# Attention's first three halves: plain fp32 products of unsplit q, k, probabilities and v, with both heads' products with v in column tiles of the array

## The chip, the cores and the metric

The kernel runs on one core of one Trainium2 chip. The metric is the device time of one execution in microseconds; runs are given as a median. PE is TensorE (PEld its weight loads), DVE VectorE, ACT ScalarE, POOL GpSimd, SP the engine that issues most DMAs.

## What is computed

Three stages follow each other on 4 x 768 = 3072 tokens: attention with sinks and a window, a feed-forward layer with a cosine, and a top-1 mixture of eight experts. All inputs are fp32.

```python
# attention: q, k, v are (4, 8, 768, 64); n_sink = 4, window = 128
scores = scale * np.matmul(q, k.transpose(0, 1, 3, 2))
keep = is_sink | in_window
a = softmax(np.where(keep, scores, -1e9))
x = np.matmul(a, v)                      # to (3072, 512)
# feed-forward, d_ff = 2048
h = x @ w_in
x = (h * np.cos(h)) @ w_out
# experts, 8 of width 1024
e = argmax(x @ w_gate + modality_bias[modality_id])
out = gate_w * (np.maximum(x @ w1[e], 0) @ w2[e])
```

## The kernel before, in words

**Halves and pairs.** Attention is worked in eight halves `hb` of 384 queries each (batch `hb // 2`, first or second part of its sequence `hb % 2`), and each half in four pairs of heads (`pr`), two heads of 64 side by side on the 128 partitions. A half has three query tiles `t` of 128. A tile sees its own block of 128 keys, the block before it, and 16 sink columns: 272 columns, and 128 for the very first tile of a sequence. A second half loads four key blocks, a first half three.

**Split products.** Matmuls work on the type fp32r, which rounds its operands. To keep fp32 precision each operand is written as a high part (ACT copies it into an fp32r tile) and a low part (DVE or POOL subtracts the high part from the value), and three products are summed in PSUM: high x high, high x low, low x high. This is done for the weights and activations of all three stages, and in attention for q, k, the probabilities and v. The transposes through PE (against `ident`) are of plain fp32, and so is the small product `pf` that spreads reciprocal sums (`mm(pf, rb[t], ident)`), which has no low parts.

**The steps of a pair** (`attn_front`, from L404):
- front: loads of q and k (L428, L429); `pq`: three transposes of q, `qT_h` by ACT and `qT_l` by DVE (L464); `pk`: transposes of k, `kT_h` by ACT (L486) and `kT_l` by DVE, then the sink keys copied behind each block (L489, L490).
- `load_v` (L431): v of the pair and its 16 sink rows `vs_n` (L436, L438). `split_v` (L494): high parts of v and of the sink rows by ACT (L497, L499), low parts by POOL, into `vp` and `vs`.
- `mid` (L515): the scores. For each tile three products per head (L136 is the helper `mm`, all products of attention and of `hp` have that line), the two heads on rows 0 to 63 and 64 to 127 of the array; DVE masks, scales and finds the row's extreme (L548), ACT takes the exponential with the row sum (L564).
- `rest` (L567): transposes of the probabilities `pt` (L588, L589), `pT_h` by ACT (L592), `pT_l` by DVE; the sink columns likewise through `pz` (L613) into `sp`; then the products with v into one PSUM bank `po`: two for the sinks and three for each block and head, with weights 128 columns wide in which the other head's 64 columns are zero. At the end the result is normalised and split into `xT_h` and `xT_l`, the input of the feed-forward stage.

From half 3 on (`STACK = 3`, L37) attention uses another, "stacked" form of these products; halves 0 to 2 use the form just described. In halves 0 and 1 the odd pairs (`extra`) hold q, k, v and the probabilities in tiles that later serve as weights of the feed-forward layer.

**Order of the work.** The feed-forward layer (`ffn_tile_gen`) runs in tiles of 384 tokens, 16 blocks `f` per tile, each of 12 products `hp` of 384 columns and 12 products `y` of 512 columns (L688); tile 0 does six blocks at first. `attn_half` (L365) yields steps with planned costs (`STEPS_0`, `STEPS_1`), and the loop at the end of attention calls `run_ffn` (L1035) after each step, so that tile `hb - 1` is spread over half `hb`. Halves 0 and 1 are piped (`PIPX`): `merge` (L342) mixes the rest of a pair with the scores of the next. Into the same order `conv_gen` (L281) weaves the conversion of the feed-forward weights, which come as 64-bit numbers: 32 blocks, each with one load by SP, work of ACT (L268, L306) and four DVE instructions (L140, L145, L148), the last of them as late as half 2. Each engine works its own queue in order, and SP issues its loads and stores in order too.

Of the kernel before, what the change touches and what calls it, by code (L numbers as in the profile page):

```python
# [11 lines left out]
F32 = DT.float32  # L12
# [8 lines left out]
P = 128  # L21
# [40 lines left out]
def kernel(  # L62
# [84 lines left out]
    def tt(e, o, a, b, op):  # L147
        e.tensor_tensor(out=o, in0=a, in1=b, op=op)  # L148
# [96 lines left out]
    kl = [kT2[:, 1]]  # L245
    ks = apool.tile([P, NPAIR, 2, NS], F32, name="ks")
    v_form = [False]
    DVE.memset(vs_n, 0.0)
    DVE.memset(vs.bitcast(F32), 0.0)
    DVE.memset(vp[:, :, D:5 * D].rearrange("p t (x d) -> p t x d", d=D)[:, :, 0:4:3].bitcast(F32), 0.0)  # L250
    POOL.memset(sp[4 * NS:].bitcast(F32), 0.0)

# [151 lines left out]
    def attn_front(hb, pr):  # L404
# [5 lines left out]

        whole = hb > EX
        n_ps = [0]

# [28 lines left out]
        qT_h = apool.tile([P, HALF], F32R, name="qT_h")  # L442
        qT_l = apool.tile([P, HALF], F32R, name="qT_l")
# [4 lines left out]
        stack = hb >= STACK  # L448
        hr = [slice(0, D), slice(D, 2 * D)]
        kT_h, kT_l = kT2[:, 0], kT2[:, 1]  # L450
        if stack:

            qT = [qT_h, qT_l]
            kx = late_pool().tile([P, 4, SEG], F32R, name="kx")
            kT = [kT_h, kx]
            if len(kl) == 1:
                kl.append(late_pool().tile([P, 4, SEG], F32R, name="kT_l1"))
                for j in range(2):
                    POOL.memset(kl[j][hr[1 - j]].bitcast(F32), 0.0)
# [10 lines left out]
        pk3 = pk.rearrange("p (t s) -> p t s", s=P)  # L470
        bs = [P, 2, nblk - 1, NS]
# [22 lines left out]
        def split_v():  # L494
            vp4 = vp.rearrange("p t (x d) -> p t x d", d=D)
            if not stack:
# [4 lines left out]
                return  # L501
            if not v_form[0]:
                v_form[0] = True
                POOL.memset(vp4[:, :, 2].bitcast(F32), 0.0)
                POOL.memset(vs[0:4 * NS].bitcast(F32), 0.0)
            ACT.activation(out=vp4[:, 0:nblk, 1:4:2, :], in_=vn[:, 0:nblk], func=AF.Copy)
# [8 lines left out]
        def mid():  # L515
            nonlocal mx, sm, Pb, Pt, cols
            kTh = kT_h.rearrange("p t s -> p (t s)")
            kTl = kT_l.rearrange("p t s -> p (t s)")
            if extra:
# [12 lines left out]
            def scores(t, js):  # L532
# [34 lines left out]
        def rest():  # L567
# [11 lines left out]
            yield steps(hb)[3]  # L579
            pT_h = apool.tile([P, 2, NQ * 256], F32R, name="pT_h")  # L580
            pT_l = apool.tile([P, 2, NQ * 256], F32R, name="pT_l")
            for t in range(NQ):
# [7 lines left out]
                oh = pT_h[:, :, t * 256 + s0:(t + 1) * 256]  # L590
                ol = pT_l[:, :, t * 256 + s0:(t + 1) * 256]
# [20 lines left out]
            for t in range(t0, NQ):  # L612
                PE.transpose(pz[0:2 * NS, t * P:(t + 1) * P], pc[:, t].rearrange("p j s -> p (j s)"), ident)  # L613
            sh, sl = sp[0:2 * NS], sp[2 * NS:4 * NS]
            if half == 0 and pr == 0:

                POOL.memset(sp[0:4 * NS, 0:t0 * P].bitcast(F32), 0.0)
            ACT.activation(out=sh[:, t0 * P:], in_=pz[0:2 * NS, t0 * P:HALF], func=AF.Copy)
            tt(DVE, sl[:, t0 * P:], pz[0:2 * NS, t0 * P:HALF], sh[:, t0 * P:].bitcast(F32), ALU.subtract)
            yield steps(hb)[5]  # L620
# [9 lines left out]
            if not stack:  # L630

                po = psb("po")
                mm(po[:, 0:HALF], vs[:, 0:2 * D], sp, True, False)
                mm(po[:, 0:HALF], vs[:, 2 * D:4 * D], sp, False, False)
                for j in range(2):
                    for blk in range(nblk):
                        c0, c1, m0, m1 = band(blk)
                        vh, vl = [vp[:, blk, (o + j) * D:(o + j + 2) * D] for o in (0, 3)]
                        mm(po[:, c0:c1], vh, pT_h[:, j, m0:m1], False, False)
                        mm(po[:, c0:c1], vh, pT_l[:, j, m0:m1], False, False)  # L640
                        mm(po[:, c0:c1], vl, pT_h[:, j, m0:m1], False, j == 1 and blk == nblk - 1)
                        yield steps(hb)[6]
                if whole:
                    ACT.activation(out=xh[:, pr, :], in_=po[:, 0:HALF], func=AF.Copy)
                    tt(DVE, xl[:, pr, :], po[:, 0:HALF], xh[:, pr, :].bitcast(F32), ALU.subtract)
                else:
# [7 lines left out]
                    tt(POOL, xl[:, pr, :], xs, xh[:, pr, :].bitcast(F32), ALU.subtract)  # L654
            if stack:
                xs = apool.tile([P, HALF], F32, name="xs")
            for j in range(2 if stack else 0):
# [241 lines left out]
    def late_pool():  # L899
        ypool_of()  # L900
        return ypl["late"]
# [546 lines left out]
```

## Time and profile before

| | us |
|---|---|
| median of 3 runs | 1201.5 (1201.12 to 1206.84) |
| the profiled execution | 1205.88 |
| its span, first to last instruction | 1204.0 |
| mean granted TensorE clock | 0.981 of 2.4 GHz |

Over the span PE is busy 1133.3 us (94%), PEld 1001.3, DVE 788.4 (65%), ACT 702.2 (58%), POOL 299.5 (25%). Matmuls are pipelined: a matmul's duration is longer than the distance to the next one's start, so busy time of PE says little about how much it could still take, and distances between starts say more. A row of a group gives the line, engine, operation, out<-in with shapes, the count, then busy time and mean ns of one, then the engine's idle time just before such instructions and who ended it. In the timeline the first two columns are the start and the time that the merged instructions cover, in us.

### The profile page before, as it was taken

The numbers are of one execution on the slowest core, as the hardware profiler recorded it, in microseconds if no ns is written. First come the engines' busy times: TensorE is split into PE (matmuls) and PEld (weight loads), VectorE is DVE, ScalarE is ACT, GpSimd is POOL, SyncE is SP. The second block draws the span as 40 slices with busy tenths as digits, with TensorE's granted clock in tenths as the row PEclk, the third lists the DMA queues.
The fourth block names the chain that finished last, engine by engine and source line by source line (L and its number), as shares of the span: only waits on it lengthen the run. The fifth ranks groups of instructions, "written<-read, shape, count | busy, mean of one in ns | idle before, by whom it ended". The sixth has DMA issues, their size and how long they took to land. (4 is left out here: it accounts for less than half of the span.)

```text
span 1204.0 us, 21827 instructions
## 1 busy us (share of the span) xinstructions
PE 1133.3 (94%) x6688; PEld 1001.3 (83%) x6688; DVE 788.4 (65%) x2293; ACT 702.2 (58%) x1453; POOL 299.5 (25%) x364
## 2 busy tenths in 40 slices
PE   5889889999999999999999999999999999999995
PEld 4777677798888898987889898989889988889984
DVE  7887879977788788788788777565762215622220
ACT  4678678777777788876788775334422225522221
POOL 1333333422322232222322222232221122122110
PEclk9889889999999999999999999999999999999998
DMA  5653456533333343333334324261333114211110
GB/s 138 159 166 117 126 167 190 149 84 79 83 93 85 78 115 79 96 95 75 75 94 114 85 54 132 78 220 54 97 130 126 38 54 137 77 53 57 37 39 24
DMA packets 141338, 118.87 MB, mean 99 GB/s; under 512 B 98415, under 2 KB 107631, under 8 KB 141168
## 3 DMA queue, kind: packets, MB, share of 16 engines
q1 hardware_dynamic: 136848, 103.29, 30.7%
q0 software_dynamic: 4320, 13.65, 3.5%
q8 instruction: 66, 1.08, 0.4%
q14 instruction: 104, 0.85, 0.3%
HBM read 151.32 MB, written 19.67 MB: 142 GB/s over the span
## 5 line engine op out<-in xcount | busy, mean ns | idle before, releaser
L148 POOL TENSOR_TENSOR g_l<-ch,g_h 128x384 fp32r<-128x384 f32 x128 | 132.0, 1032 | 424.4 <-ACT g_h L760 394.4
L136 PE MATMUL hp<-xT_h,wi_h 128*128 128x384 f32 x512 | 182.1, 356 | 0.0
L136 PE MATMUL hp<-xT_h,wi_l 128*128 128x384 f32 x512 | 174.6, 341 | 0.0
L136 PE MATMUL hp<-xT_l,wi_h 128*128 128x384 f32 x512 | 174.4, 341 | 0.0
L688 PE MATMUL y<-wo,g_h 128*128 128x512 f32 x384 | 161.0, 419 | 0.0
L688 PE MATMUL y<-wo_l,g_h 128*128 128x512 f32 x384 | 158.2, 412 | 0.0
L688 PE MATMUL y<-wo,g_l 128*128 128x512 f32 x384 | 155.9, 406 | 0.2 <-POOL g_l L148 0.2
L145 DVE SCALAR_TENSOR_TENSOR hT<-m_h,hT 128x256 fp32r<-128x256 f32 x88 | 37.3, 424 | 151.2 <-ACTq L1346 95.0
L136 PE MATMUL m_y<-wi_h,hT 128*128 128x512 f32 x416 | 132.4, 393 | 0.6 <-issue 0.4
L750 ACT ACTIVATE ch<-ch,cols 128x384 f32<-128x384 f32 x128 | 78.9, 616 | 85.2 <-DVE ch L145 84.0
L136 PEld LDWEIGHTS hp<-xT_h,wi_h 128*128 128x128 f32 x512 | 97.4, 190 | 4.9 <-issue 0.6
L142 DVE TENSOR_SCALAR ch<-hp 128x384 int32<-128x384 f32 x128 | 71.1, 555 | 45.1 <-PE hp L136 30.2
L136 PEld LDWEIGHTS hp<-xT_l,wi_h 128*128 128x128 f32 x512 | 97.5, 190 | 3.7 <-issue 0.4
L136 PEld LDWEIGHTS hp<-xT_h,wi_l 128*128 128x128 f32 x512 | 97.1, 190 | 0.6 <-issue 0.2
L136 PEld LDWEIGHTS m_y<-wi_h,hT 128*128 128x128 f32 x416 | 78.1, 188 | 16.9 <-issue 0.8
L564 ACT ACTIVATE Pb<-Pb,mx 128x272 f32<-128x272 f32 (+1 forms) x168 | 82.8, 494 | 12.7 <-DVE mx L548 12.0
L760 ACT ACTIVATE g_h<-ch 128x384 fp32r<-128x384 f32 x128 | 66.4, 519 | 40.5 <-DVE ch L148 32.0
L148 DVE TENSOR_TENSOR ch<-ch,hp 128x384 f32<-128x384 f32 x128 | 70.2, 550 | 28.4 <-ACT ch L750 26.8
L1163 ACT ACTIVATE hT<-m_h 128x256 fp32r<-128x256 f32 x88 | 33.8, 384 | 88.4 <-PE m_h L136 81.3
L688 PEld LDWEIGHTS y<-wo,g_l 128*128 128x128 f32 x384 | 73.3, 191 | 14.0 <-POOL g_l L148 0.6
L136 PE MATMUL m_y<-wi_l,hT 128*128 128x512 f32 x208 | 81.0, 390 | 0.0
L688 PEld LDWEIGHTS y<-wo,g_h 128*128 128x128 f32 x384 | 73.5, 192 | 8.7 <-issue 0.5
(306 smaller groups left out, 2821.8 us busy)
## 6 DMA issues: line engine op xcount, KB each, us to landing
rw<-in_moe_w_dram SPq DMA_DIRECT2D x112, 512.0 KB
wo_l<-wl_scr SPq DMA_DIRECT2D x122, 256.0 KB
cv_in<-in_moe_w_in_dram SPq DMA_DIRECT2D x16, 512.0 KB
cv_out<-in_moe_w_out_dram SPq DMA_DIRECT2D x16, 512.0 KB
y_scr<-yt SPq DMA_DIRECT2D x24, 256.5 KB
xT_h<-xg_h SPq DMA_DIRECT2D x32, 192.0 KB
xT_l<-xg_l SPq DMA_DIRECT2D x32, 192.0 KB
qn<-in_q_dram SPq DMA_DIRECT2D x56, 96.0 KB
```

Source lines behind the costliest of these rows:

```text
L136: PE.matmul(o, l, r, start=start, stop=stop)
L142: e.tensor_scalar(out=o, in0=i, scalar1=s1, scalar2=s2, op0=op0, op1=op1)
L145: e.scalar_tensor_tensor(out=o, in0=i0, scalar=s, in1=i1, op0=op0, op1=op1)
L148: e.tensor_tensor(out=o, in0=a, in1=b, op=op)
L564: ACT.activation(out=Pb[t][j][:, c0:c1], in_=Pb[t][j][:, c0:c1], func=AF.Exp, scale=-1.0, bias=mx[:, i:i + 1], accum_out=sm[:, i:i + 1])
L688: i = PE.matmul(o, l, r, start=start, stop=stop)
L750: ACT.activation(out=ch, in_=ch, func=AF.Sin, scale=TWO_PI, bias=half_pi)
L760: ACT.activation(out=gh, in_=ch, func=AF.Copy)
L1163: ACT.activation(out=hT_h[f], in_=hp, func=AF.Relu)
```

## The change

In halves 0, 1 and 2 (`stack` false) q, k, the probabilities, the sink columns and v stay whole, in fp32 tiles. Scores are one fp32 product per tile and head instead of three fp32r products. For the products with v the heads no longer share weights of 128 columns: head j has weights of 64 columns, `vn` as it was loaded, and writes partitions 64 j to 64 j + 63 of `po`. `split_v` does nothing in these halves. q, k, the probabilities and the sink rows have two buffers by turns (they use the places of the high and low tiles), v has three in the even pairs. The tiles of the stacked form are made when half 3 begins (`stacked`), in the same places. The yields keep their planned costs.

```diff
-    vp = apool.tile([P, 4, 6 * D], F32R, name="vp")
-    vs = apool.tile([P, 4 * D], F32R, name="vs")
-    vs_n = apool.tile([4 * NS, 2 * D], F32, name="vs_n")
-    sp = apool.tile([P, HALF], F32R, name="sp")
-    kT2 = apool.tile([P, 2, 4, SEG], F32R, name="kT_hl")
...
+    vs_n = apool.tile([P, 2 * D], F32, name="vs_n")
...
+    vn3 = apool.tile([P, 3, 4, 2, D], F32, name="vn3", tag="vp")
+    vs_n1 = apool.tile([P, 2 * D], F32, name="vs_n1", tag="vs")
+    spf = apool.tile([P, HALF], F32, name="spf", tag="sp")
+    kf2 = apool.tile([P, 2, 4, SEG], F32, name="kf", tag="kT_hl")
+    DVE.memset(vs_n1, 0.0)
+    POOL.memset(spf, 0.0)
+    st_ = {}
+
+    def stacked():
+        if not st_:
...
         def load_v():
           nonlocal vn
-          if not extra:
-              vn = apool.tile([P, 4, 2, D], F32, name="vn")
+          if vn is None:
+              vn = apool.tile([P, 4, 2, D], F32, name="vn") if stack else vn3[:, pr % 3]
           for j in range(2):
...
-            for g_ in range(2):
-                SP.dma_start(out=vs_n[(2 * g_ + j) * NS:(2 * g_ + j + 1) * NS, j * D:(j + 1) * D], in_=v[b, h0 + j, 0:NS, :])
+            for g_ in range(2 if stack else 1):
+                SP.dma_start(out=vn_s[(2 * g_ + j) * NS:(2 * g_ + j + 1) * NS, j * D:(j + 1) * D], in_=v[b, h0 + j, 0:NS, :])
...
+            qf = apool.tile([P, HALF], F32, name="qf", tag=("qT_h", "qT_l")[pr % 2])
+            kf_ = kf2[:, pr % 2]
...
-            ACT.activation(out=qT_h, in_=pq[:, 0:HALF], func=AF.Copy)
-            tt(DVE, qT_l, pq[:, 0:HALF], qT_h.bitcast(F32), ALU.subtract)
+            ACT.activation(out=qf, in_=pq[:, 0:HALF], func=AF.Copy)
...
-            ACT.activation(out=kT_h[:, 0:nblk, 0:P], in_=pk3[:, 0:nblk, :], func=AF.Copy)
-            tt(DVE, kT_l[:, 0:nblk, 0:P], pk3[:, 0:nblk, :], kT_h[:, 0:nblk, 0:P].bitcast(F32), ALU.subtract)
-            if half == 0:
-                DVE.tensor_copy(ks[:, pr], kT2[:, :, 0, 0:NS].bitcast(F32))
-            DVE.tensor_copy(kT2[:, :, 0:nblk - 1, P:SEG], ks[:, pr].unsqueeze(2).to_broadcast(bs))
+            ACT.activation(out=kf_[:, 0:nblk, 0:P], in_=pk3[:, 0:nblk, :], func=AF.Copy)
+            if half == 0 and hb + 1 < STACK:
+                DVE.tensor_copy(ks[:, pr, 0], pk3[:, 0, 0:NS])
+            if half == 0 and hb + 1 >= STACK:
+                DVE.tensor_copy(ks[:, pr, 0].bitcast(F32R), pk3[:, 0, 0:NS])
+                tt(DVE, ks[:, pr, 1], pk3[:, 0, 0:NS], ks[:, pr, 0], ALU.subtract)
+            src = pk3[:, 0:1, 0:NS] if half == 0 else ks[:, pr, 0:1, :]
+            DVE.tensor_copy(kf_[:, 0:nblk - 1, P:SEG], src.to_broadcast([P, nblk - 1, NS]))
...
         def split_v():
+            if not stack:
+                return
...
-                ACT.activation(out=vp4[:, 0:nblk, 0:3:2], in_=vn[:, 0:nblk], func=AF.Copy)
-                tt(POOL, vp4[:, 0:nblk, 3:6:2], vn[:, 0:nblk], vp4[:, 0:nblk, 0:3:2].bitcast(F32), ALU.subtract)
-                ACT.activation(out=vs[0:4 * NS, 0:2 * D], in_=vs_n, func=AF.Copy)
-                tt(POOL, vs[0:2 * NS, 2 * D:4 * D], vs_n[0:2 * NS], vs[0:2 * NS, 0:2 * D].bitcast(F32), ALU.subtract)
...
-                    for n_, (q_, k_) in enumerate(((qT_h, kTh), (qT_h, kTl), (qT_l, kTh))):
-                        for j in js:
-                            mm(ps[j][:, 0:w], q_[hr[j], qs], k_[hr[j], o:o + w], n_ == 0, n_ == 2)
+                    for j in js:
+                        mm(ps[j][:, 0:w], qf[hr[j], qs], kfr[hr[j], o:o + w], True, True)
...
-                ACT.activation(out=oh, in_=pt[:, :, s0:256], func=AF.Copy)
-                tt(DVE, ol, pt[:, :, s0:256], oh.bitcast(F32), ALU.subtract)
...
+                pT = apool.tile([P, 2, NQ * 256], F32, name="pT", tag=("pT_h", "pT_l")[pr % 2])
...
+                    ACT.activation(out=pT[:, :, o_], in_=pt[:, :, s0:256], func=AF.Copy)
...
+                ACT.activation(out=spf[0:2 * NS, t0 * P:], in_=pz[0:2 * NS, t0 * P:HALF], func=AF.Copy)
...
                 po = psb("po")
-                mm(po[:, 0:HALF], vs[:, 0:2 * D], sp, True, False)
-                mm(po[:, 0:HALF], vs[:, 2 * D:4 * D], sp, False, False)
                 for j in range(2):
-                    for blk in range(nblk):
-                        c0, c1, m0, m1 = band(blk)
-                        vh, vl = [vp[:, blk, (o + j) * D:(o + j + 2) * D] for o in (0, 3)]
-                        mm(po[:, c0:c1], vh, pT_h[:, j, m0:m1], False, False)
-                        mm(po[:, c0:c1], vh, pT_l[:, j, m0:m1], False, False)
-                        mm(po[:, c0:c1], vl, pT_h[:, j, m0:m1], False, j == 1 and blk == nblk - 1)
-                        yield steps(hb)[6]
+                    mm(po[hr[j], 0:HALF], vn_s[:, j * D:(j + 1) * D], spf, True, False)
+                for blk in range(nblk):
+                    c0, c1, m0, m1 = band(blk)
+                    for j in range(2):
+                        mm(po[hr[j], c0:c1], vn[:, blk, j, :], pT[:, j, m0:m1], False, blk == nblk - 1)
+                    yield 2 * steps(hb)[6]
```

## Rows read from the trace of the kernel before

**Rows 1.** The page, the span in 40 equal slices: busy tenths of PE and DVE.

```profile
PE   5889889999999999999999999999999999999995
DVE  7887879977788788788788777565762215622220
```

**Rows 2.** Busy time by stretch: PE, PEld, DVE, ACT, POOL (counts), PE clock, DMA share, GB/s.

```profile
12.00:70.00 58.00, 47.95 (x263) 39.94 (x264) 49.04 (x151) 40.53 (x118) 15.60 (x30) 0.94 0.60 156
70.00:142.00 72.00, 63.09 (x383) 53.46 (x380) 58.80 (x126) 54.78 (x117) 26.89 (x46) 0.91 0.42 128
142.00:257.00 115.00, 106.45 (x582) 88.83 (x583) 95.72 (x235) 84.48 (x174) 41.19 (x58) 0.94 0.53 156
257.00:355.00 98.00, 94.99 (x567) 84.38 (x567) 79.97 (x240) 76.66 (x149) 25.51 (x28) 1.00 0.35 88
```

**Rows 3.** Groups of instructions by form, DVE, 12 to 250 us.

```profile
L148 DVE TENSOR_TENSOR pT_l<-pt,pT_h 128x512 fp32r<-128x512 f32 x28 | 19.0, 684 | 2.6 <-ACT pT_h L592 2.5
...
L148 DVE TENSOR_TENSOR qT_l<-pq,qT_h 128x384 fp32r<-128x384 f32 x12 | 6.6, 548 | 0.0
...
L148 DVE TENSOR_TENSOR kT_hl<-pk,kT_hl 128x384 fp32r<-128x384 f32 x8 | 4.4, 549 | 0.4 <-ACT kT_hl L486 0.4
L148 DVE TENSOR_TENSOR pT_l<-pt,pT_h 128x256 fp32r<-128x256 f32 x8 | 3.3, 416 | 0.0
...
L148 DVE TENSOR_TENSOR kT_hl<-pk,kT_hl 128x512 fp32r<-128x512 f32 x4 | 2.8, 690 | 0.2 <-ACT kT_hl L486 0.2
...
L148 DVE TENSOR_TENSOR sp<-pz,sp 32x128 fp32r<-32x128 f32 x8 | 2.2, 280 | 0.3
...
L148 DVE TENSOR_TENSOR sp<-pz,sp 32x384 fp32r<-32x384 f32 x4 | 2.2, 548 | 0.1
```

**Rows 4.** The same view, ACT, 12 to 250 us.

```profile
L499 ACT ACTIVATE vs<-vs_n 64x128 fp32r<-64x128 f32 x12 | 3.7, 306 | 5.4 <-issue 3.9 <-POOL pc L608 0.9 <-DMA ld_x<-in_k_dram 0.5
L497 ACT ACTIVATE vp<-vn 128x384 fp32r<-128x384 f32 x6 | 3.1, 521 | 2.3 <-PE po L136 2.2
```

**Rows 5.** The same view, POOL, 12 to 250 us.

```profile
L148 POOL TENSOR_TENSOR vp<-vn,vp 128x384 fp32r<-128x384 f32 x6 | 6.6, 1105 | 20.5 <-DMA ld_x<-in_q_dram 14.0 <-ACT vp L497 4.2 <-DMA wo_l<-wl_scr 2.1
```

**Rows 6.** Waits of SP's queue, 12 to 250 us: total, times, longest in us.

```profile
SPq L438 <- POOL vs L148: 21.4, 8, 7.2
```

**Rows 7.** Timeline of PE around the scores of one tile in half 2.

```profile
228.85 0.39 PE L688 MATMUL y<-wo_l,g_h 128*128 128x512 f32 x1
229.07 0.40 PE L688 MATMUL y<-wo,g_l 128*128 128x512 f32 x1
229.40 0.52 PE L136 MATMUL ps<-kT_hl,qT_h 64*128 64x272 f32 x4
229.76 0.29 PE L136 MATMUL ps<-kT_hl,qT_l 64*128 64x272 f32 x2
229.97 0.45 PE L136 MATMUL hp<-xT_h,wi_h 128*128 128x384 f32 x1
230.26 0.34 PE L136 MATMUL hp<-xT_l,wi_h 128*128 128x384 f32 x1
```

**Rows 8.** Timeline of PE around the products with v of one pair in half 2.

```profile
194.59 0.33 PE L136 MATMUL hp<-xT_h,wi_h 128*128 128x384 f32 x1
194.76 0.34 PE L136 MATMUL hp<-xT_l,wi_h 128*128 128x384 f32 x1
...
195.12 0.51 PE L136 MATMUL po<-sp,vs 128*128 128x384 f32 x2
195.46 0.28 PE L136 MATMUL po<-pT_h,vp 128*128 128x256 f32 x1
195.58 0.28 PE L136 MATMUL po<-pT_l,vp 128*128 128x256 f32 x1
```

**Rows 9.** Timeline of PE at the plain fp32 products of one pair in half 1.

```profile
134.97 0.83 PE L136 MATMUL pf<-ident,pb_x 128*128 128x128 f32 x6
```

**Rows 10.** All plain fp32 products of that kind: duration in ns, smallest, median, largest.

```profile
L136 PE MATMUL pf<-ident,pb_x x48: 270/275/377, 36.1 to 135.5; 128*128 128x128 f32 x48
```

More of the change, by code (lines that the diff above doesn't have):

```diff
@@ L235 @@
     apool = att.enter_context(tc.tile_pool(name="apool", bufs=1, side="right"))
-    vp = apool.tile([P, 4, 6 * D], F32R, name="vp")
-    vs = apool.tile([P, 4 * D], F32R, name="vs")
-    vs_n = apool.tile([4 * NS, 2 * D], F32, name="vs_n")
-    sp = apool.tile([P, HALF], F32R, name="sp")
-    kT2 = apool.tile([P, 2, 4, SEG], F32R, name="kT_hl")
-    kl = [kT2[:, 1]]
+    vs_n = apool.tile([P, 2 * D], F32, name="vs_n")
     ks = apool.tile([P, NPAIR, 2, NS], F32, name="ks")
-    v_form = [False]
     DVE.memset(vs_n, 0.0)
-    DVE.memset(vs.bitcast(F32), 0.0)
-    DVE.memset(vp[:, :, D:5 * D].rearrange("p t (x d) -> p t x d", d=D)[:, :, 0:4:3].bitcast(F32), 0.0)
-    POOL.memset(sp[4 * NS:].bitcast(F32), 0.0)
+    vn3 = apool.tile([P, 3, 4, 2, D], F32, name="vn3", tag="vp")
[7 more added lines that the diff above has]
+        if not st_:
+            vp = apool.tile([P, 4, 6 * D], F32R, name="vp", tag="vp")
+            vs = apool.tile([P, 4 * D], F32R, name="vs", tag="vs")
+            sp = apool.tile([P, HALF], F32R, name="sp", tag="sp")
+            kT2 = apool.tile([P, 2, 4, SEG], F32R, name="kT_hl", tag="kT_hl")
+            kl1 = late_pool().tile([P, 4, SEG], F32R, name="kT_l1")
+            st_.update(vp=vp, vs=vs, sp=sp, kT=kT2[:, 0], kl=[kT2[:, 1], kl1])
+            for j in range(2):
+                POOL.memset(st_["kl"][j][(1 - j) * D:(2 - j) * D].bitcast(F32), 0.0)
+            POOL.memset(vp[:, :, 2 * D:3 * D].bitcast(F32), 0.0)
+            POOL.memset(vs.bitcast(F32), 0.0)
+            POOL.memset(sp[4 * NS:].bitcast(F32), 0.0)
+        return st_
     def conv_in(cpool, f):
@@ L411, in attn_front @@
         whole = hb > EX
+        stack = hb >= STACK
+        vn_s = vs_n1 if not stack and pr % 2 else vs_n
         n_ps = [0]
@@ L447, in attn_front @@
             PE.transpose(pq[:, t * P:(t + 1) * P], qn[:, t].rearrange("p j d -> p (j d)"), ident)
-        stack = hb >= STACK
         hr = [slice(0, D), slice(D, 2 * D)]
-        kT_h, kT_l = kT2[:, 0], kT2[:, 1]
         if stack:
             qT = [qT_h, qT_l]
[L454 to L459, printed above, removed]
+            kl = stacked()["kl"]
+            kT = [stacked()["kT"], late_pool().tile([P, 4, SEG], F32R, name="kx")]
             for j in range(2):
@@ L470, in attn_front @@
         pk3 = pk.rearrange("p (t s) -> p t s", s=P)
-        bs = [P, 2, nblk - 1, NS]
         bj = [D, nblk - 1, NS]
@@ L494, in split_v @@
         def split_v():
+            if not stack:
+                return
+            vp, vs = stacked()["vp"], stacked()["vs"]
             vp4 = vp.rearrange("p t (x d) -> p t x d", d=D)
-            if not stack:
-                ACT.activation(out=vp4[:, 0:nblk, 0:3:2], in_=vn[:, 0:nblk], func=AF.Copy)
-                tt(POOL, vp4[:, 0:nblk, 3:6:2], vn[:, 0:nblk], vp4[:, 0:nblk, 0:3:2].bitcast(F32), ALU.subtract)
-                ACT.activation(out=vs[0:4 * NS, 0:2 * D], in_=vs_n, func=AF.Copy)
-                tt(POOL, vs[0:2 * NS, 2 * D:4 * D], vs_n[0:2 * NS], vs[0:2 * NS, 0:2 * D].bitcast(F32), ALU.subtract)
[L501 to L505, printed above, removed]
             ACT.activation(out=vp4[:, 0:nblk, 1:4:2, :], in_=vn[:, 0:nblk], func=AF.Copy)
@@ L516, in mid @@
             nonlocal mx, sm, Pb, Pt, cols
-            kTh = kT_h.rearrange("p t s -> p (t s)")
-            kTl = kT_l.rearrange("p t s -> p (t s)")
+            kfr = None if stack else kf_.rearrange("p t s -> p (t s)")
             if extra:
@@ L579, in rest @@
             yield steps(hb)[3]
-            pT_h = apool.tile([P, 2, NQ * 256], F32R, name="pT_h")
-            pT_l = apool.tile([P, 2, NQ * 256], F32R, name="pT_l")
+            if stack:
+                pT_h = apool.tile([P, 2, NQ * 256], F32R, name="pT_h")
+                pT_l = apool.tile([P, 2, NQ * 256], F32R, name="pT_l")
+            else:
+                pT = apool.tile([P, 2, NQ * 256], F32, name="pT", tag=("pT_h", "pT_l")[pr % 2])
             for t in range(NQ):
@@ L589, in rest @@
                     PE.transpose(pt[:, j, P:2 * P], Pb[t][j][:, SEG:W3], ident)
-                oh = pT_h[:, :, t * 256 + s0:(t + 1) * 256]
-                ol = pT_l[:, :, t * 256 + s0:(t + 1) * 256]
-                ACT.activation(out=oh, in_=pt[:, :, s0:256], func=AF.Copy)
-                tt(DVE, ol, pt[:, :, s0:256], oh.bitcast(F32), ALU.subtract)
+                o_ = slice(t * 256 + s0, (t + 1) * 256)
+                if stack:
+                    ACT.activation(out=pT_h[:, :, o_], in_=pt[:, :, s0:256], func=AF.Copy)
+                    tt(DVE, pT_l[:, :, o_], pt[:, :, s0:256], pT_h[:, :, o_].bitcast(F32), ALU.subtract)
+                else:
+                    ACT.activation(out=pT[:, :, o_], in_=pt[:, :, s0:256], func=AF.Copy)
                 yield steps(hb)[4]
@@ L613, in rest @@
                 PE.transpose(pz[0:2 * NS, t * P:(t + 1) * P], pc[:, t].rearrange("p j s -> p (j s)"), ident)
-            sh, sl = sp[0:2 * NS], sp[2 * NS:4 * NS]
+            sp = stacked()["sp"] if stack else None
             if half == 0 and pr == 0:
-                POOL.memset(sp[0:4 * NS, 0:t0 * P].bitcast(F32), 0.0)
-            ACT.activation(out=sh[:, t0 * P:], in_=pz[0:2 * NS, t0 * P:HALF], func=AF.Copy)
-            tt(DVE, sl[:, t0 * P:], pz[0:2 * NS, t0 * P:HALF], sh[:, t0 * P:].bitcast(F32), ALU.subtract)
+                POOL.memset((sp[0:4 * NS, 0:t0 * P].bitcast(F32) if stack else spf[0:2 * NS, 0:t0 * P]), 0.0)
+            if stack:
+                sh, sl = sp[0:2 * NS], sp[2 * NS:4 * NS]
+            if stack:
+                ACT.activation(out=sh[:, t0 * P:], in_=pz[0:2 * NS, t0 * P:HALF], func=AF.Copy)
+                tt(DVE, sl[:, t0 * P:], pz[0:2 * NS, t0 * P:HALF], sh[:, t0 * P:].bitcast(F32), ALU.subtract)
+            else:
+                ACT.activation(out=spf[0:2 * NS, t0 * P:], in_=pz[0:2 * NS, t0 * P:HALF], func=AF.Copy)
             yield steps(hb)[5]
@@ L632, in rest @@
                 po = psb("po")
-                mm(po[:, 0:HALF], vs[:, 0:2 * D], sp, True, False)
-                mm(po[:, 0:HALF], vs[:, 2 * D:4 * D], sp, False, False)
                 for j in range(2):
-                    for blk in range(nblk):
-                        c0, c1, m0, m1 = band(blk)
-                        vh, vl = [vp[:, blk, (o + j) * D:(o + j + 2) * D] for o in (0, 3)]
-                        mm(po[:, c0:c1], vh, pT_h[:, j, m0:m1], False, False)
-                        mm(po[:, c0:c1], vh, pT_l[:, j, m0:m1], False, False)
-                        mm(po[:, c0:c1], vl, pT_h[:, j, m0:m1], False, j == 1 and blk == nblk - 1)
-                        yield steps(hb)[6]
+                    mm(po[hr[j], 0:HALF], vn_s[:, j * D:(j + 1) * D], spf, True, False)
+                for blk in range(nblk):
+                    c0, c1, m0, m1 = band(blk)
+                    for j in range(2):
+                        mm(po[hr[j], c0:c1], vn[:, blk, j, :], pT[:, j, m0:m1], False, blk == nblk - 1)
+                    yield 2 * steps(hb)[6]
                 if whole:
@@ L655, in rest @@
             if stack:
+                vp, vs = stacked()["vp"], stacked()["vs"]
                 xs = apool.tile([P, HALF], F32, name="xs")
```

6 lines of the change are left out of this document (4 added, 2 removed).

## The prediction

> **What bounds the kernel now.** I began with the slices of the page [rows 1]: PE is busy nine tenths or more from a fifth of the span on, and before that it has holes, while DVE stands at seven to nine tenths. The changed halves (hb 0, 1 and 2 of eight) all lie in this first fifth, so the rest of the kernel can only move as a block. The table by stretch [rows 2] cuts that fifth at the places where the work changes. In 12 to 70 us half 0 runs nearly without FFN work; in 70 to 142 half 1 runs beside FFN tile 0, cut to six blocks; in 142 to 257 half 2 runs beside a whole FFN tile; 257 to 355 is the first stretch whose half is not touched, again beside one whole tile. Busy PE time overlaps in a pipeline, so I priced PE by starts. The 567 matmuls of 257 to 355 fill 98 us at clock 1.00: 0.17 us each, so that stretch is PE's. In 12 to 70 there are 263, mostly small ones that start 0.11 apart: 29 us of work in 58. In 70 to 142 there are 383 at about 0.13: 50 us in 72. There PE is not the limit; DVE has 49.0 of 58 and 58.8 of 72 us, 82 to 85%, as near to full as an in-order engine gets in chains like these. ACT has 70 and 76%. In 142 to 257 one tile and one half take 115 us where the next take 98, with DVE at 95.7 and the clock at 0.94. So 17 us is all that this stretch could give.
>
> **What goes.** Each split of a value into two parts costs DVE a subtraction. Gone are 28 + 8 for the probabilities, 12 for q, 8 + 4 for k and 8 + 4 for the sink columns [rows 3]: 19.0 + 3.3 + 6.6 + 4.4 + 2.8 + 2.2 + 2.2 = 40.5 us of DVE. Per pair of heads that is 0.55 + 0.55 + 0.42 + 2 x 0.68 + 0.28 = 3.2 us in halves 0 and 2, and 0.55 + 0.69 + 3 x 0.68 + 0.55 = 3.8 in half 1. The copies of sink keys (L489, L490) only change their source and stay. The first stretch also holds the front of half 1's first pair, which the second lacks. So DVE falls from 49.0 to 35 us, from 58.8 to 44 and from 95.7 to 83. ACT loses the copies of v, 12 of 0.52 or a little more and 12 of 0.31 [rows 4], some 10 us in all, POOL the subtractions behind them, over 1 us each [rows 5]. On POOL I cost this at nothing: it is idle more than half of each stretch [rows 2].
>
> **Waits moved.** SP now waits 21.4 us in eight waits for POOL to be done with the sink rows of v before it may load the next [rows 6], and every later load queues behind it, raw weights for the conversion among them. That wait goes with the split. What is late next is PE: v and its sink rows are read by the products themselves, so their buffers come free only when the pair's last product is done. Three buffers of v and two of sink rows cover that in half 2; in halves 0 and 1 odd pairs share one buffer two pairs apart, whose products were issued a pair earlier. I take it as even, between a gain of the 21.4 us of SP time (which no engine has been seen to wait for) and a loss of the 7.2 us of the longest wait. The second buffers of q, k and the probabilities can only help. Two loads of sink rows per pair fewer, and fills on POOL and DVE before the first product, I cost at nothing beside the loads that everything awaits at the start.
>
> **What comes, on PE.** Before: three products per tile and head, both heads at once in the two row halves of the array: four starts of a 272-column product up to 229.76 and two more, until 229.97 [rows 7], 0.12 per pair of products. Entering and leaving costs about 0.1 each: 0.33 before the first against 0.23 between FFN products, and 0.29 behind the next one against 0.17 [rows 7, 8]. A product of plain fp32 is two instructions: six for three products of 128 columns [rows 9], start to start (0.83 - 0.275) / 5 = 0.11 us [rows 9, 10], so 0.22 per 128 columns. At 128 columns this may be a floor, since the split products of 256 columns start 0.12 apart as well [rows 8]; the ends are therefore 0.12 and 0.24 for an instruction of 272 columns. I take 0.24, since the row of plain fp32 is the only one of its kind. The Trainium skill, FP8 and Floating Point Precision, section TensorE Precision Notes, has true fp32 pass the array four times; by that rule the high end is right, by the low end the second case below would hold.
> Scores: four instructions in order, the second head's first beside the first head's second, make a chain of three: 0.71 us against 0.36 for 272 columns, equal for 128. Per pair that is +0.70 in halves 0 and 2, +1.05 in half 1.
> Products with v, before: two sinks in 0.34, then 0.12 for 256 columns and at most 0.11 for 128 [rows 8]: 18 in half 0 (12 and 6), 2.4 us; 24 in half 1, 3.1. After, an instruction costs 0.33, 0.22 or 0.11 for 384, 256 or 128 columns: 3.55 us for the 16 of half 0 in a row, 4.0 for the 20 of half 1. The heads sit in two column tiles; no row shows such a pair, so the cost lies between half of that and all of it. I take three quarters (a chain of three for four, as with the scores), plus 0.2 per entry into the tile shape, four to five times as FFN products come between: 3.5 and 4.0, so +1.05 and +0.9.
> Per half of four pairs: +7.0, +7.7 and +7.0 us of PE, 22 in all, with ends of about 0 and 33.
>
> **The sum.** 12 to 70: DVE 35, ACT 37 and PE 36 of 58; chains set the pace, and of DVE's 14 us I count half, **-7**. 70 to 142: PE at 58, ACT at 51, DVE at 44; PE is now the limit, at 88% of its time 66, **-5** (one of them lost to the clock, 0.91 here). 142 to 257: 98 as in the next stretch plus 7 is 105 at best; the conversion still loads DVE with 83, I take 111, **-4**. From 257 us on nothing changes. The profiled execution has 1205.9 us, 1204.0 of it span; 16 off makes 1189.9. It lies 4.4 above the median of 1201.5, and the forecast on the median's footing is **1186**.
>
> **Rivals.**
> *Cheap products:* fp32 at the low end and column tiles side by side. PE gets nothing more to do; ACT's 37 and 51 us at 76 and 81% of the time leave 49 and 63 (-9, -9), half 2 gives half of its 17 (-8): 1175. For it: both prices rest on bounds; against it: the only fp32 row.
> *Relief unused:* column tiles one after the other, PE +10, +12 and +10. ACT's 37 us and the chain of steps hold the first stretch (-2), the second gives 1 and the third 0: 1198. For it: ACT at 70 to 76% already; against it: DVE's higher share in both stretches.
> *Slower, by exposed weight loads:* column tiles use all rows, so if a tile's weights load only when the other's product has left the rows, each of the 16 or 20 instructions adds a load, 53.46 / 380 = 0.14 us [rows 2], on top of one after the other. Per half of four pairs +19, +23 and +19 us: 70 to 142 needs 73 us of PE, 81 at 90%; 142 to 257 needs 117 and 122 with its dips of the clock; the first stretch gains 0. That is +9 and +7: 1217. It decides once a pair's products with v take over about 5 us. Against it: full-height products start 0.17 and 0.12 apart [rows 8], which leaves no room for 0.14 us of load between them, so there loads overlap.
> The Trainium skill, TensorE: Matmul & The Clock Gate, section The mechanism under Part 3, lets weight loads overlap running products only where the row groups differ; by that rule this last case holds, and the rows of full-height products speak against it.
>
> **Chances.** Forecast 0.48, cheap products 0.18, relief unused 0.20, slower 0.14. A measurement of this kernel can tell about 0.5%, 6 us, from no change. The first two lie beyond that, and a little of the third: faster 0.67, same 0.20, slower 0.13. The range leaves out the slower case and the outer half of the cheap one: 1171 to 1206.
>
> **What would show it.** Right: DVE near 35, 44 and 83 us in these stretches; instructions of 272-column scores 0.24 apart with the heads side by side in the middle; po instructions in pairs with nearly equal starts; half 1's last products some 10 us earlier; from 257 on a shift only. Wrong: po instructions strictly one after another; a stretch of half 2 longer than 115 us; SP waiting for po where it waited for POOL; a gain that the later stretches give back.

## The result and the profile after

The changed kernel takes **1173.5 us** (median of 4 runs, 1170.7 to 1176.4) against 1201.3 of the kernel before (4 runs beside them): ratio 0.976, 95% interval 0.973 to 0.979, so 28 us or 2.4% faster. The profiled execution has a span of 1174.5 us; with 1176.4 us it is the slowest of the four, so its tables lean a few us to the slow side. Differences between kernels below are differences of such ratios times 1201.3 us, since every kernel was timed beside the kernel before on its own chip; a ratio is uncertain by some 0.2 to 0.3%, about 3 us, and a difference of two ratios by some 4 us.

The page of the changed kernel, the span in 40 equal slices, busy tenths of PE and DVE [rows 1]:

```profile
PE   5999999999999999999999999999999998999995
DVE  5668779687878887788887785656652124612210
```

The holes of PE in the second to sixth slice are gone. The table by stretch of the changed kernel, cut at the same places of the work as [rows 2] (columns as there: PE, PEld, DVE, ACT, POOL, clock, DMA share, GB/s):

```profile
12.00:60.00 48.00, 45.42 (x232) 29.15 (x233) 33.64 (x119) 36.04 (x104) 8.24 (x21) 1.00 0.59 152
60.00:116.00 56.00, 52.99 (x324) 39.22 (x324) 42.22 (x105) 47.98 (x107) 15.79 (x36) 0.97 0.65 193
116.00:227.00 111.00, 107.45 (x548) 79.32 (x547) 86.28 (x226) 85.13 (x174) 37.15 (x53) 0.98 0.55 163
227.00:325.00 98.00, 94.94 (x568) 84.46 (x567) 79.61 (x238) 76.71 (x149) 25.75 (x28) 1.00 0.35 88
```

Against 58, 72, 115 and 98 us the stretches now take 48, 56, 111 and 98: -10, -16, -4 and 0. The whole gain lies before 227 us. DVE and ACT have less to do, POOL too, and PE is busy 95 to 97% of these three stretches where it was 83 to 93%. The last of the eight products of po by the normalising factors in halves 0 and 1 shows the same shift (durations in ns, first and last start in us; the kernel before, then the changed one):

```profile
L148 DVE TENSOR_TENSOR xs<-po,xs x8: 544/546/558, 39.1 to 142.7; 128x384 f32<-128x384 f32 x8
```

```profile
L148 DVE TENSOR_TENSOR xs<-po,xs x8: 548/554/558, 34.6 to 114.6; 128x384 f32<-128x384 f32 x8
```

So half 1 ends 28 us earlier. **PE's instructions** at the first pair of half 0, first the kernel before, then the changed one (timeline of PE: start, us, what, count):

```profile
33.62 0.62 PE L136 MATMUL po<-sp,vs 128*128 128x384 f32 x2 [1.44 <-DVE sp L148]
34.08 0.28 PE L136 MATMUL po<-pT_h,vp 128*128 128x256 f32 x1
...
36.12 0.66 PE L136 MATMUL pf<-ident,pb_x 128*128 128x128 f32 x4
```

```profile
31.11 0.87 PE L136 MATMUL po<-spf,vs_n 128*64 128x384 f32 x4
31.80 1.25 PE L136 MATMUL po<-pT,vn 128*64 128x256 f32 x12
32.98 0.38 PE L136 MATMUL pf<-ident,pb_x 128*128 128x128 f32 x1
```

Twenty split instructions took 36.12 - 33.62 = 2.50 us, the sixteen plain ones take 32.98 - 31.11 = 1.87. They start in pairs: in the records behind the last group one head's instruction starts at 31.801 and the other head's at 31.807, the next two at 32.017 and 32.023, so 0.216 us for a pair of 256 columns, and 0.109 for a pair of 128 (32.664 to 32.773). Each instruction has the high price of the prediction (0.22 and 0.11), but the second head's costs next to nothing. The weight loads lie under the products:

```profile
31.80 1.01 PEld L136 LDWEIGHTS po<-pT,vn 128*64 128x64 f32 x10 [0.18 <-issue]
```

Ten loads between 31.80 and 32.81, while the products run from 31.80 to 32.98. The scores of one tile in half 2 [rows 7] now run

```profile
198.97 0.40 PE L700 MATMUL y<-wo,g_l 128*128 128x512 f32 x1
199.29 0.73 PE L136 MATMUL ps<-kf,qf 64*128 64x272 f32 x4
199.95 0.44 PE L136 MATMUL hp<-xT_h,wi_h 128*128 128x384 f32 x1
```

in 0.66 us, 0.09 more than the 229.97 - 229.40 = 0.57 of before.

### The profile page after: what moved, and what is told of

The parts are those of the page before. It is cut to its first block, busy times and chain, and to the rows that moved or that the text cites. A ratio compares the mean times of both kernels' runs of the same rounds, so it can differ in the third digit from the quotient of the medians.

```text
span 1174.5 us, 21326 instructions
## 1 busy us (share of the span) xinstructions
PE 1121.5 (95%) x6560; PEld 967.7 (82%) x6560; DVE 745.4 (63%) x2224; ACT 691.2 (59%) x1427; POOL 277.3 (24%) x341
## 5 line engine op out<-in xcount | busy, mean ns | idle before, releaser
L148 DVE TENSOR_TENSOR ch<-ch,hp 128x384 f32<-128x384 f32 x128 | 70.2, 550 | 31.1 <-ACT ch L762 29.7
L1206 ACT ACTIVATE m_ot<-m_y,m_yg 128x512 f32<-128x512 f32 x26 | 17.9, 689 | 106.7 <-PE m_y L136 106.0
```

What stands on the lines that cost most here:

```text
L1206: ACT.activation(out=m_ot[h], in_=yp, func=AF.Copy, scale=m_yg[i][h][:, DM:YC])
```

## The experiments

**1. Only VectorE's subtractions away, from the kernel before.** The low parts of q, k, probabilities and sinks in halves 0 to 2 are zeros, written once; all products stay.

```
-            tt(DVE, qT_l, pq[:, 0:HALF], qT_h.bitcast(F32), ALU.subtract)
-            tt(DVE, kT_l[:, 0:nblk, 0:P], pk3[:, 0:nblk, :], kT_h[:, 0:nblk, 0:P].bitcast(F32), ALU.subtract)
...
-                tt(DVE, ol, pt[:, :, s0:256], oh.bitcast(F32), ALU.subtract)
+                if stack:
+                    tt(DVE, ol, pt[:, :, s0:256], oh.bitcast(F32), ALU.subtract)
```

> The kernel before with its split products, but in halves 0 to 2 the low parts of q, k, the probabilities and the sink columns are left out: they are zeros written once at the start, so DVE does none of the 40.5 us of subtractions and PE issues the same products as before. If DVE's relief gives the time (theory A), most of the 28 us comes here too: 1173 to 1183 us. If the time comes from PE's own work, the plain fp32 products and the clock that goes with them (theory B), it stays at 1193 to 1201. If it comes from second buffers and from v that is no longer split (theory C), it is 1190 to 1200 as well.

Measured: 1192.9 us, ratio 0.993 (0.991 to 0.995), -8.5 us. Its table in the stretches of [rows 2]:

```profile
12.00:70.00 58.00, 49.58 (x293) 41.17 (x293) 38.39 (x132) 41.61 (x121) 18.14 (x35) 0.97 0.55 144
70.00:142.00 72.00, 65.40 (x377) 54.93 (x377) 49.40 (x115) 56.46 (x119) 25.77 (x43) 0.87 0.53 155
```

DVE has some 10 us less in each, and the gain is under a third of the 28: theory A does not hold.

**2. The same subtractions put back into the changed kernel,** into a tile that nothing reads. To make room for it v of half 2 has two buffers instead of three, as in run 3.

```
+            tt(DVE, lo[:, 0:HALF], pq[:, 0:HALF], qf, ALU.subtract)
...
+                    tt(DVE, lo.rearrange("p (j x) -> p j x", j=2)[:, :, s0:256], pt[:, :, s0:256], pT[:, :, o_], ALU.subtract)
```

> The changed kernel with the 40.5 us of DVE subtractions put back, in the same places and shapes, into a tile that nothing reads (v of half 2 then has two buffers instead of three). Theory A: the gain is lost, 1193 to 1202 us. Theories B and C: 1174 to 1182.

Measured: 1181.5 us, 0.982 (0.979 to 0.985), 7.4 us over the changed kernel. Both ways round, VectorE's relief is worth some 8 us.

**3. The split of v by ScalarE and GpSimd put back,** also into an unread tile.

```
+                ACT.activation(out=h4, in_=vn[:, 0:3], func=AF.Copy)
+                tt(POOL, h4, vn[:, 0:3], h4, ALU.subtract)
```

> The changed kernel with the split of v put back at its old place, into a tile that nothing reads: the high parts of v (three blocks) and of its sink rows by ACT, the low parts by POOL, 9 us of ACT and about 18 us of POOL in all (v of half 2 has two buffers). So far DVE's relief is worth 8 to 9 of 28 us. If most of the rest comes from v that no longer goes through ACT and POOL (theory C1), this is at 1184 to 1194 us. If those engines have room (theory D: the rest is PE's own time), 1173 to 1178.

Measured: 1177.9 us, 0.980 (0.977 to 0.982), +4.6 us, about as much as two such ratios can tell apart.

**4. Split scores, plain products with v.** q and k are split and multiplied as before the change, and with that have one buffer each again; the probabilities keep two.

```
-            qf = apool.tile([P, HALF], F32, name="qf", tag=("qT_h", "qT_l")[pr % 2])
-            kf_ = kf2[:, pr % 2]
+        qT_h = apool.tile([P, HALF], F32R, name="qT_h")
+        qT_l = apool.tile([P, HALF], F32R, name="qT_l")
+        kT_h, kT_l = kT2s[:, 0], kT2s[:, 1]
...
-                    for j in js:
-                        mm(ps[j][:, 0:w], qf[hr[j], qs], kfr[hr[j], o:o + w], True, True)
+                    for n_, (q_, k_) in enumerate(((qT_h, kTh), (qT_h, kTl), (qT_l, kTh))):
+                        for j in js:
+                            mm(ps[j][:, 0:w], q_[hr[j], qs], k_[hr[j], o:o + w], n_ == 0, n_ == 2)
```

> The changed kernel with the split scores of before (q and k in two parts, three products, single buffers), products with v plain. DVE gets 13.8 of its 40.5 us back, PE loses about 0.1 us per tile of 272 columns. Theory A: a third of the gain goes, 1180 to 1186 us. Theory B: 1172 to 1177.

Measured: 1176.3 us, 0.978 (0.976 to 0.980), +2.5 us over the changed kernel, inside what the intervals leave open. But the buffers differ, so this is not the price of the scores alone. The fair base is run 7 below, with the same buffers and plain scores: 1169.1 us, 0.973 (0.971 to 0.975). Against it the split scores cost 6.4 us, and the intervals do not touch. TensorE's time for the scores is about the same in both forms (30.5 us before, 30.7 in the changed kernel, worked out below), so VectorE's subtractions for q and k are the likely cause; that was not tried alone.

**5. The heads' products with v one after the other,** all of head 0 before head 1, the same instructions.

```
-                for blk in range(nblk):
-                    c0, c1, m0, m1 = band(blk)
-                    for j in range(2):
+                    for blk in range(nblk):
+                        c0, c1, m0, m1 = band(blk)
```

> The changed kernel with the products with v of head 0 all issued before those of head 1, so that no two column tiles can run side by side. If side by side is what made them cheap, the instructions start 0.21 us apart for 256 columns, a pair of heads takes 1.7 to 2 us more on PE, and with PE now the limit in halves 1 and 2 the kernel is at 1182 to 1190 us. If PE still has room there: 1173 to 1177. If the column tiles were never side by side, no start changes and neither does the time.

Measured: 1188.1 us, 0.989 (0.986 to 0.991), 15.3 us over the changed kernel. In its timeline a pair of half 0 begins and ends so:

```profile
38.28 0.86 PE L136 MATMUL po<-spf,vs_n 128*64 128x384 f32 x2
...
41.28 0.94 PE L136 MATMUL pf<-ident,pb_x 128*128 128x128 f32 x6
```

3.00 us where side by side took 1.87. Summed over the three halves from start to next start, at the higher clock and without waits: 208 instructions at a mean of 0.202 us are 41.9 us, against 208 at 0.129 = 26.8 in the changed kernel and 264 at 0.123 = 32.5 before. The 15.1 us of TensorE between the first two match the 15.3 us of time.

**6. One buffer each for q, k and the probabilities,** as before the change, instead of two.

```
-            qf = apool.tile([P, HALF], F32, name="qf", tag=("qT_h", "qT_l")[pr % 2])
-            kf_ = kf2[:, pr % 2]
+            qf = apool.tile([P, HALF], F32, name="qf", tag="qT_h")
+            kf_ = kf2[:, 0]
...
-                pT = apool.tile([P, 2, NQ * 256], F32, name="pT", tag=("pT_h", "pT_l")[pr % 2])
+                pT = apool.tile([P, 2, NQ * 256], F32, name="pT", tag="pT_h")
```

> The changed kernel with one buffer each for q, k and the probabilities of halves 0 to 2 instead of two by turns. If the second buffers carry the rest of the gain (theory C2), 1184 to 1194 us; if not, 1173 to 1177.

Measured: **1164.0 us, 0.968 (0.966 to 0.970)**, 9.1 us under the changed kernel, faster than both, and outside both cases of the expectation. The second pair's products with v show one thing that differs. The changed kernel, timeline of PE:

```profile
35.17 0.86 PE L136 MATMUL po<-spf,vs_n 128*64 128x384 f32 x2
35.96 0.73 PE L136 MATMUL ps<-kf,qf 64*128 64x128 f32 x4
...
37.84 0.73 PE L136 MATMUL ps<-kf,qf 64*128 64x272 f32 x4
38.50 0.65 PE L136 MATMUL po<-pT,ld_x 128*64 128x256 f32 x4
39.11 0.72 PE L136 MATMUL ps<-kf,qf 64*128 64x272 f32 x2
39.76 0.43 PE L136 MATMUL po<-pT,ld_x 128*64 128x128 f32 x2
40.12 0.38 PE L136 MATMUL pf<-ident,pb_x 128*128 128x128 f32 x1
```

and with one buffer:

```profile
37.74 0.87 PE L136 MATMUL po<-spf,vs_n 128*64 128x384 f32 x4
38.44 1.25 PE L136 MATMUL po<-pT,ld_x 128*64 128x256 f32 x12
39.62 0.94 PE L136 MATMUL pf<-ident,pb_x 128*128 128x128 f32 x6
```

With two buffers the next pair's scores are free to go, and stand in PE's order between this pair's products: 40.12 - 35.17 = 4.95 us to the next product behind them instead of 39.62 - 37.74 = 1.88. The pair starts earlier and ends later.

That this makes the 9.1 us is not shown. It is one pair of twelve: the fourth pair of half 0 has scores among its products in both forms, and in halves 1 and 2 no pair has any, in either form. The clock has a part as well: its mean is 0.991 to 0.995 in the four runs of the changed kernel and 0.994 to 0.997 here, some 3.5 us of full rate. In the two profiled executions, 15.4 us apart, the last FFN product starts at 838.8 and 827.0 us; the last 3.7 us arise behind it, where the two kernels have the same code and the execution of the changed kernel had two spells of 1.2 GHz more (from 989 and from 1010 us).

**7. Two buffers of the probabilities alone.**

```
-                pT = apool.tile([P, 2, NQ * 256], F32, name="pT", tag="pT_h")
+                pT = apool.tile([P, 2, NQ * 256], F32, name="pT", tag=("pT_h", "pT_l")[pr % 2])
```

> The changed kernel with one buffer for q and k as before the change, but two for the probabilities. If it is the early scores of the next pair (let go by the second buffers of q and k) that cost 9.5 us: 1162 to 1166, as with one buffer of each. If it is the second buffer of the probabilities, by which the transposes of the next pair come in among this pair's products with v: 1171 to 1176, as in the changed kernel. If each has a share: between.

Measured: 1169.1 us, 0.973 (0.971 to 0.975), 5.3 us over one buffer of each and 3.8 under the changed kernel. So the second buffer of the probabilities costs time, the intervals just apart; a share of the second buffers of q and k lies inside the intervals. In this trace the second pair's products stand together, without scores between them (from 38.56 us on), and 5.3 us are lost all the same: the scores at that place are not the whole cause, and what the rest is stays open.

**8. A pair's products with v in one go,** with no step between them at which FFN products are let in; and **9. the same on the one-buffer form.** The edit is the same line moved out of the loop over blocks:

```
-                    yield 2 * steps(hb)[6]
+                yield 2 * nblk * steps(hb)[6]
```

> The changed kernel with all products with v of a pair issued without FFN products between them (the planned steps follow in one). PE then changes its tile shape once per pair instead of three or four times, at about 0.2 us each time: if PE is now the limit in halves 1 and 2 (theory D), 1167 to 1171 us. If the products between them filled a wait, or PE has room, 1173 to 1178.

Measured: 1170.7 us, 0.975 (0.972 to 0.978), 1.3 us less by the ratios (2.8 by the medians), inside the intervals. In half 0 the next pair's scores still come in between: the second pair's products run from 32.63 to 37.58 us, as long as without the edit. So this run says nothing of what those scores cost.

> The one-buffer form of the changed kernel (1164.0 us), with all products with v of a pair issued without FFN work between them, which alone took 2.8 us from the changed kernel. If the two effects add: 1160 to 1163. If the products in one go only helped because pairs overlapped (two buffers): 1163 to 1167, no better than the one-buffer form.

Measured: 1164.2 us, 0.969 (0.967 to 0.972), no better than the one-buffer form alone. Whatever 8 brought does not add to it, as the second case had it.

**10. TensorE's instructions of before, without any low part worked out,** on the one-buffer form. The products that took low parts read the high part again or zeros; the copy of v by ScalarE is back, in two buffers, and v itself and its sink rows, as loaded, have one buffer instead of several.

```
-                    mm(po[hr[j], 0:HALF], vn_s[:, j * D:(j + 1) * D], spf, True, False)
-                for blk in range(nblk):
-                    c0, c1, m0, m1 = band(blk)
-                    for j in range(2):
-                        mm(po[hr[j], c0:c1], vn[:, blk, j, :], pT[:, j, m0:m1], False, blk == nblk - 1)
+                    for blk in range(nblk):
+                        c0, c1, m0, m1 = band(blk)
...
+                        mm(po[:, c0:c1], vw, pT[:, j, m0:m1], False, False)
+                        mm(po[:, c0:c1], vw, z[:, 0:c1 - c0], False, False)
+                        mm(po[:, c0:c1], vw, z[:, 256:256 + c1 - c0], False, j == 1 and blk == nblk - 1)
```

> The one-buffer form (1164.0 us) with TensorE's instructions of the kernel before put back and nothing else: q, k, probabilities and sinks are written once, as fp32r, by ScalarE; the scores are three fp32r products for each head, and the products with v are three 128-column fp32r products for each head and block one head after the other, with the low parts replaced by the high part again or by zeros, so no low part is ever worked out (v is copied once by ScalarE; VectorE's and GpSimd's subtractions stay away). Theory A, TensorE's side by side plain products give what VectorE's relief leaves over: 1178 to 1190. Theory B, the relief of VectorE, ScalarE and GpSimd gives nearly all and the form of TensorE's products nothing: 1163 to 1168. Time at the lower clock: by A some spells come back, by B none.

Measured: 1182.2 us, 0.984 (0.982 to 0.987). Theory A: with the other engines relieved alike, the form of TensorE's products (with ScalarE's one copy of v and v's buffers) makes 1.62% or 19.5 us. Its first three stretches, then those of the one-buffer form:

```profile
12.00:60.00 48.00, 42.20 (x242) 35.27 (x242) 34.44 (x116) 37.88 (x109) 9.29 (x21) 0.96 0.71 182
60.00:116.00 56.00, 53.55 (x315) 45.28 (x315) 34.89 (x95) 45.06 (x105) 15.12 (x34) 0.88 0.47 142
116.00:227.00 111.00, 103.86 (x612) 88.59 (x611) 89.89 (x218) 87.38 (x183) 34.18 (x52) 0.97 0.59 168
```

```profile
12.00:60.00 48.00, 44.55 (x243) 28.37 (x243) 35.48 (x126) 38.30 (x111) 11.39 (x25) 1.00 0.62 160
60.00:116.00 56.00, 55.40 (x339) 40.76 (x338) 45.03 (x116) 49.71 (x109) 18.21 (x34) 1.00 0.71 207
116.00:227.00 111.00, 108.01 (x580) 82.50 (x579) 90.25 (x233) 89.27 (x182) 38.49 (x53) 1.00 0.56 163
```

From the clock column, at half speed in what is missing to 1.00, the split form loses 0.04 x 48 + 0.12 x 56 + 0.03 x 111 = 12 us of TensorE's full rate and the plain form nothing. From start to next start its products with v take 264 x 0.121 = 31.9 us against 208 x 0.126 = 26.2, the scores about the same (28.7 and 29.1). 12 + 5.7 - 0.4 is 17 of the 19.5 us. This is an estimate from one execution of each, and it counts a us of lost rate as a us of time.

**11. The plain form in all eight halves.** In halves 2 to 6 the last pair's products read the v of the next half's first pair, which has the same buffer, so the numbers that come out are wrong; the instructions are those of the plain form.

```
-STACK = 3
+STACK = 8
```

> The changed kernel with the plain form in all eight halves instead of three. In halves 3 to 7 PE is the limit already. The plain form costs PE there 0.47 us per tile of scores beside 0.50 for the stacked form, and as much for the products with v, plus changes of tile shape of about 0.2 us, six to seven per pair: 20 pairs by 1.0 to 1.4 us would make 1194 to 1202 us. If the time follows DVE and ACT as in halves 0 to 2, it is faster, 1160 to 1170.

Measured: 1198.2 us, 0.996 (0.995 to 0.998), 24.5 us over the changed kernel. Not all of it is the plain form's: in the profiled executions, 24.4 us apart, the last FFN product starts at 857.9 us against 838.8, and the other 5 us arise in the experts' stage, whose input is another here. So against the two-head form of halves 3 to 7, where TensorE is the limit already, plain products cost about 19 us, nearly 4 a half.

## Why the prediction was right, and where it was not

The sign and the order of size were right, 1173.5 in a range of 1171 to 1206, but 28 us came where 16 were forecast, and that the time lies in the range, 2.5 us from its lower end, is luck in part: two errors worked against each other. TensorE got less to do where more was forecast, and the second buffers, put at no cost, took 9 us back; with one buffer each the change lands at 1164 us, below the range.

- **What goes, DVE:** right. 33.6, 42.2 and 86.3 us were measured for 35, 44 and 83. What it is worth was put too high. The sum drew all of its gain from VectorE's relief, against more work on PE; alone, with PE's products as before, it brings 7 to 9 us (runs 1, 2). That POOL's part costs nothing may have been too strict: it and ACT's bring 4.6 us (run 3), at the edge of what the ratios can tell.
- **What comes, on PE:** the step that failed is "a chain of three for four", three quarters of serial, for two heads in two column tiles. The price of an instruction was right (0.216 us for 256 columns, forecast 0.22), but the heads overlap wholly, so it is half of serial. For scores too the heads start side by side: four instructions of 272 columns take 0.66 us with entry and exit, +0.09 where +0.35 was forecast. The products with v went from 32.5 to 26.8 us, the scores from 216 x 0.141 = 30.5 to 144 x 0.213 = 30.7 (these two move by about a us with the length from which a gap counts as a wait): TensorE got 5.5 us less to do, where the sum had 22 more. Run 5 is the sum's serial case made real, and its 15 us show up in full.
- **The sum, stretch by stretch:** -10, -16 and -4 for -7, -5 and -4. The middle one failed, as PE was put at 58 us there and so at its limit. With PE's price mended it is not, as the cheap-products case had it (-9, -9, -8, total 1175). That case came nearest in time, but for other reasons: of its two conditions the tiles side by side came and the low price of fp32 did not. Run 10 comes close to what it describes, the other engines relieved and nothing new for PE, and gives 18.7 us where it had 26; the other 19.5 come from the form of PE's products, which no case had as a gain. The third stretch behaved as the forecast's; that conversion still loads DVE with 86 us there fits, but was not tried alone.
- **Second buffers "can only help":** wrong, by 9.1 us (run 6), the largest error after PE's price. It hid in the total: without it the change is worth 38 us. One thing that they do is seen in the second pair: a buffer is also a gate, and opening it let later work in among the work that others wait for. How the 9.1 us come about is open.
- **A term that the sum lacked: the clock.** [Rows 2] have 0.94, 0.91 and 0.94, the stretches after 1.00, 0.97 and 0.98. At half speed in what is missing, 0.06 x 58 + 0.09 x 72 + 0.06 x 115 = 17 us of full rate were lost before, 0 + 0.03 x 56 + 0.02 x 111 = 4 after. The table by stretch around one fall in the kernel before, and around one in the changed kernel:

```profile
141.00:144.40 3.40, 1.11 (x7) 0.93 (x7) 3.40 (x6) 2.15 (x6) 1.53 (x2) 1.00 0.76 231
144.40:154.60 10.20, 10.20 (x34) 6.51 (x34) 7.21 (x24) 7.23 (x13) 0.76 (x1) 0.50 0.52 126
```

```profile
118.80:122.20 3.40, 1.49 (x8) 0.94 (x8) 3.33 (x14) 2.41 (x5) 0.00 (x0) 1.00 0.39 89
122.20:125.60 3.40, 3.40 (x11) 1.89 (x9) 2.38 (x6) 3.38 (x10) 0.00 (x0) 0.50 0.62 165
```

In both, PE had been busy for a third to a half of the time before, waiting; then it is busy all the time at 1.2 GHz. So in both places slow time follows a wait of PE. How much of the 13 us came straight into the time was not tried alone. The runs of the kernel before bear on it: the fastest on record took 1197.7 us at a mean clock of 0.988, the slowest 1208.6 at 0.976, some 15 us of full rate for 11 us of time, though the waits themselves are in that too.
- **What the clock column leaves out.** It has no record before 31.8 us in the kernel before and 30.0 in the changed one, and counts that time as 1.00. But PE's transposes of 128 columns take 421 ns there and 272 to 273 just after, as at 1.2 and 2.4 GHz elsewhere. So [rows 2] make half 0 look faster on PE than it was, and the prediction's "29 us of work in 58" prices at 2.4 GHz what ran at 1.2 for a third of that stretch. The two kernels lose nearly the same there. Between executions it varies: the changed kernel and runs 3, 5, 7, 8 and 11 have the same PE instructions in the same order up to the first products with v, yet the clock rose between 23.6 and 30.0 us and these products began between 28.6 and 31.1. So two single traces can differ by 2 us before their kernels differ at all.
- **Waits moved:** SP waits where it was foretold. The queue's waits of the changed kernel, 12 to 227 us (total, times, longest):

```profile
SPq L452 <- PE po L136: 17.5, 8, 4.8
SPq L450 <- PE po L136: 3.4, 5, 1.7
```

20.9 us for PE where 21.4 were for POOL [rows 6]: even, as taken. The text's sign of a wrong prediction, "SP waiting for po", appeared and cost nothing that shows; as a sign it was badly chosen.
- **Exposed weight loads,** the slower rival: did not come. The loads lie under the products (10 in the 1.01 us above). The Trainium skill, TensorE: Matmul & The Clock Gate, section The mechanism under Part 3, has loads overlap running products only where the row groups differ; the trace does not agree, since full-height column tiles share their rows and their loads overlap all the same. The same section also lets a load into the background weight buffer run ahead, which the prediction left out.
- **From 257 us on a shift only:** right. The untouched stretch takes 98 us again.

By steps, in ratios: relief of the other engines with TensorE's instructions as before takes 18.7 us (run 10 against before, of which VectorE alone is 8.5), the plain form of the products another 19.5 (run 6 against run 10), and the second buffers give 9.1 back: 29.1, the change. What makes 18.7 out of VectorE's 8.5 and the 4.6 of v's split is open in part: run 10 also has v's copies in two buffers.

## What to carry to other kernels

Price two products that go to separate column tiles as one, and try it in the order that puts them next to each other: the order alone was worth 15 us here. Add a buffer only after asking what in-order work the single one holds back, and time it; the unchanged number of buffers beat the changed kernel by 9 us, and **1164 us with one buffer each is the version to keep.** Where the granted clock of a stretch lies below 1.00, look at the idle time of TensorE just before, and check where the record begins: here the kernel with fewer waits also spent less time at 1.2 GHz (34 us before and 7 after, in the first 200 us as far as the clock is on record).

## What was not expected of the hardware

- Plain fp32 products into two column tiles, each 128 rows by 64 columns, start 6 to 7 ns apart, and a pair costs 0.216 us for 256 columns and 0.109 for 128, as much as one alone would at the prediction's high price. The Trainium skill, FP8 and Floating Point Precision, section TensorE Precision Notes, has true fp32 pass the array four times; the trace comes near that: the two instructions of a plain product take 0.43 us, 3.6 times the 0.12 of a split product of 256 columns [rows 8].
- Going into the column tiles and out again costs about 0.1 us each time, as with the scores' row tiles. Timeline of PE in half 2 of the changed kernel:

```profile
188.91 0.40 PE L700 MATMUL y<-wo_l,g_h 128*128 128x512 f32 x1
189.15 0.40 PE L700 MATMUL y<-wo,g_l 128*128 128x512 f32 x1
189.47 0.87 PE L136 MATMUL po<-spf,vs_n 128*64 128x384 f32 x4
190.17 0.60 PE L136 MATMUL po<-pT,vn 128*64 128x256 f32 x4
190.70 0.50 PE L700 MATMUL y<-wo,g_h 128*128 128x512 f32 x1
```

From the last FFN product to the first sink product 0.32 us, where the FFN product before took 0.24 (189.15 - 188.91); and of the 0.53 from 190.17 to 190.70, two pairs of 0.216 account for 0.43.
